# Gated mix of linear attention and a Fourier layer: q' as seven products of quarters, x's forms made once

## The chip, the core and the metric

The kernel runs on one core of a Trainium2 chip. Five engines work side by side: TensorE (PE, matmuls; PEld is its weight load), VectorE (DVE), ScalarE (ACT), GpSimd (POOL) and SyncE (SP). SP and POOL issue nearly all transfers here. Times are device microseconds from runs on the chip; lower is better. What is asked: by how much the change moves the time of 729.68 us.

## The reference

With S = 2048 rows, D = 576 columns, H = 32 heads of 18 columns:

```python
g = sigmoid((x * gate_w).sum(-1, keepdims=True))
q, k, v = split((x @ wqkv))                    # heads of 18
phi = lambda t: where(t > 0, t + 1, exp(t)) + 1e-6
kv  = einsum("bhsd,bhse->bhde", phi(k), v)
z   = einsum("bhsd->bhd", phi(k))
o   = einsum("bhqd,bhde->bhqe", phi(q), kv) / (phi(q) . z + 1e-6)
a   = o.reshape(S, D) @ wo
b   = Cr @ (x @ Wr.T) - Ci @ (x @ Wi.T)        # real part of the 2-D DFT, given as matrices
out = g * a + (1 - g) * b
```

All is fp32. The kernel holds fp32 accuracy in fp32r matmuls: each operand is split into a high part (rounded by a copy) and a low part (the difference), and a product is high x high + high x low + low x high, three passes.

## The kernel before

The rows of x lie in 16 tiles of 128 (NT); D is 4 full chunks of 128 and a rest of 64, whose rows are stored twice so that two passes do for it instead of three. A plain product of one tile and half of the columns (HALF = 288) is therefore 4 x 3 + 2 = 14 matmuls (`steps`, line 272).

The stages, in order of time:

1. **k'** (lines 445 to 562). phi(x Wk) for 16 tiles, in halves. The first four tiles (FT) go through the chunks together while the weights arrive (L502); the other twelve tile by tile (`k_half`, L206 for the matmul). `feature` (L341) takes each half out of its bank: Relu and Exp on ScalarE (L343, L344), an addition on VectorE (L345). `k_split` (L462) splits the tile to high and low (L464). x arrives as `xraw` (L259) and is split by `split_next` (`hi_of`, L176, on ScalarE; `lo_of`, L186, on VectorE).
2. **Attention sums** (lines 565 to 674). G = x^T phi(k), L626, in 20 steps of 4 tiles; kv from Wv and G (`kv_step`, L608 and L611); z from the sum of the phi(k) (`z_chain`, `z_sum`).
3. **q'** (`q_tile`, L677). 16 tiles x 2 halves x 14 matmuls. x is loaded and split a second time. Wq has two more columns, the gate's; `q_tile` takes the gate from the bank of the second half. Beside it run `normalise` (L696, the denominators and the division), `build_m` (L762, M = kv Wo) and `move_m`.
4. **The M stage** (lines 1109 to 1143). Each tile of the attention output is transposed by TensorE (`transposed`, L724), split, multiplied by M in 28 matmuls, scaled by the gate (L1116) and stored as `att`.
5. **Spectral part** (`Hidden.run`, L899, then `sequence`, L1010; twice, for the real and the imaginary matrix). Its products use a scheme of seven products of quarters in place of eight: x of two tiles (p and p + 8) and W are cut to quarters, sums of quarters are formed, and seven products give four quarters of the result. The seven left operands are called the forms of x, the seven right ones the forms of W. A product of forms is 2 x 3 + 1 = 7 matmuls (L896).

The forms of x are made by `Left` (L352): load four quarters, four sums, high and low parts, store to DRAM (`xforms`, L386). Nine of them (8 pairs and the rests) are made here and there: four in k', two in the attention sums, three in the M stage. The forms of W come from `right` (L402), which makes them in three pieces and stores them in DRAM; `Hidden.load_w` (L861) loads them again.

The order: VectorE and ScalarE follow the program text (`pace`), SP too. TensorE's order was left to the framework's planner up to the spectral part and follows the text from there (line 1181). Work that shall come later in the text is kept in lists (`pending`, `tick`). PSUM has eight banks of 512 columns (`bank`).

Of the kernel before, what the change touches and what calls it, by code (L numbers as in the profile page):

```python
# [30 lines left out]

# [15 lines left out]

# [27 lines left out]
QH = HALF, HALF + 2  # L75


LAY_Q = dict(xs=(-256, 4864, 9984, 43776), hi=(15104, 20864), lo=(26688, 31296))
# [3 lines left out]
ORDER = (3, 2, 7, 6, 1, 4, 5)  # L82
MIX_AT = ACC_AT
# [3 lines left out]
XF = 4 * P * 4  # L87


class Layout:  # L90

# [43 lines left out]
def kernel(  # L135
# [6 lines left out]
    wq: bass.AP,  # L142
    wv: bass.AP,
# [35 lines left out]
    pending, paced = [], ExitStack()  # L179

# [67 lines left out]
    raws, split = [], []  # L248
    order = []
    xs_ring = Ring(0, 0, 0)  # L250

    def new_xs(name="xs", ring=xs_ring):
        o = ring.next()
        return (at(o, [P, 10, P], R, name), at(o + XS // 2, [P, 5, P], F, "xraw"))

    def load_next():
        if order:
            xs, raw = new_xs()
            nc.sync.dma_start(out=raw, in_=xa[order.pop(0)])  # L259
            raws.append((xs, raw))  # L260

    def split_next(lo_of=lo_of):
        if raws:
            xs, raw = raws.pop(0)
            hi_of(xs[:, 0:5], raw)
            lo_of(xs[:, 5:10], raw, xs[:, 0:5])
            split.append(xs)

    def x_at(lay):
        xs_ring.at, xs_ring.n = [SLOT_AT + o for o in lay["xs"]], 0  # L270

# [8 lines left out]

    def split_wide(t, c, raw):
        hi_of(t[:, c], raw)
        if c < KC:
            lo_of(t[:, 5 + c], raw, t[:, c])
        else:
            lo_of(t[64:, c], raw[64:], t[64:, c])
# [3 lines left out]
    class Wide:  # L290
# [6 lines left out]
        def load(self, h, pieces=(KC,), queues=None, also=lambda k: None):  # L297
# [5 lines left out]
            for k in pieces:  # L303
                o = self.start + self.lay["lo"][h] + c * n * 4
                los.append((c, at(o, [P, k, n], R, "wd"), at(o, [P, k, n], F, "wraw")))
                c += k
# [9 lines left out]
        def split(self, h, n=1, lo_of=lo_of):  # L316

            hi, los, rest = self.got[h]
            for c, lo, raw in los:
                k = lo.shape[1]  # L320
                m = max(k * n // KC, 1)
                for a in range(0, k, k // m):
                    cs = slice(a, a + k // m)
                    hs = slice(c + a, c + a + k // m)
                    hi_of(hi[:, hs], raw[:, cs])
                    lo_of(lo[:, cs], raw[:, cs], hi[:, hs])
                    yield
            hi_of(hi[:, KC], rest)
            lo_of(hi[64:, KC], rest[64:], hi[64:, KC])
            yield  # L330
# [8 lines left out]
    es = Ring(Y_AT, 1184, 3)  # L339

    def feature(dst, ps):  # L341
        e = at(es.next(), [P, HALF], F, "e")
        nc.scalar.activation(e, ps, AF.Relu, scale=-1.0)  # L343
        nc.scalar.activation(e, e, AF.Exp, scale=-1.0)  # L344
        nc.vector.scalar_tensor_tensor(dst, ps, 0.0, e, op0=ALU.max, op1=ALU.add)  # L345


# [4 lines left out]
    class Left:  # L352

        def __init__(self, k, start, after):
            self.k = k
            if k < NP:
                self.f, self.c = (at(start, [P, 7, 2, 2 * P], d, "xb") for d in (F, R))
                for i in range(2):  # L360
                    begin_after(nc.gpsimd.dma_start(out=self.f[:, 4 * i + 1:4 * i + 3, 1],
                                                    in_=xq[k, :, 2 * i:2 * i + 2]), after)
# [3 lines left out]
            for i in range(4):  # L366
                begin_after(nc.gpsimd.dma_start(
                    out=self.f[:, (1, 2, 5, 6)[i], 1],
# [116 lines left out]
    for _ in range(3):  # L485
        load_next()
# [792 lines left out]
```

## Time and profile before

| what | us |
|---|---|
| three runs | 729.1, 729.68, 730.55 |
| median | 729.68 |
| span of the profiled execution (first to last instruction) | 727.9 |
| PE busy in it | 723.1 |
| DVE busy | 600.3 |
| ACT busy | 335.5 |
| POOL busy | 57.1 |

The profiled execution has no time of its own besides its span; the median of the runs is 1.8 us above the span. In the profile, a busy time is the time in which an engine worked on at least one instruction. Instructions of one engine may overlap a little, so a sum of durations can be above the busy time. A chain of waits is followed back from the last instruction to what released each step. Bytes in the issues are KB of one transfer.

### The profile page before, as it was taken

How to read it: one execution, taken by the hardware profiler on the slowest of the kernel's cores; microseconds unless marked ns; L12 is line 12 of the kernel's file. 1: busy time of each engine (PE TensorE's matmuls, PEld its weight loads, DVE VectorE, ACT ScalarE, POOL GpSimd, SP SyncE). 2: the span in 40 equal slices, each digit the busy share in tenths (PEclk: the TensorE clock that was granted, in tenths of full speed). 3: DMA queues.
4: the chain of work that ended last, by engine and by line, in shares of the span. 5: the costliest groups of instructions: out<-in, count | busy, mean ns of one | idle time of the engine just before them, and what ended most of it. 6: DMA issues, size and time to landing. Idle time of an engine off the chain costs nothing.

```text
span 727.9 us, 13874 instructions
## 1 busy us (share of the span) xinstructions
PE 723.1 (99%) x5446; PEld 722.0 (99%) x5446; DVE 600.3 (82%) x994; ACT 335.5 (46%) x521; POOL 57.1 (8%) x98
## 2 busy tenths in 40 slices
PE   9999999999999999999999999999999999999997
PEld 9999999999999999999999999999999999999997
DVE  5689877689999948989989989857889988788884
ACT  6898346678643544453434333323435322232330
POOL 1011300051132110000000000000000000000000
PEclk9999999999999999999999999999999999999999
DMA  7376796676477999644475666889954443544440
GB/s 255 91 274 220 266 332 199 221 219 230 147 257 279 365 331 380 182 163 144 147 263 168 225 233 199 306 281 402 377 206 135 168 148 124 163 151 140 152 152 33
DMA packets 54228, 158.83 MB, mean 218 GB/s; under 512 B 6412, under 2 KB 10828, under 8 KB 53140
## 3 DMA queue, kind: packets, MB, share of 16 engines
q1 hardware_dynamic: 44916, 118.90, 48.2%
q0 software_dynamic: 8960, 38.65, 14.6%
q8 instruction: 43, 0.70, 0.4%
q10 hardware_dynamic: 288, 0.41, 0.2%
q14 instruction: 21, 0.17, 0.1%
HBM read 115.06 MB, written 41.39 MB: 215 GB/s over the span
## 4 chain that ended last, share of the span: by engine, by line
PE 99%; DVE 0%; DVEq 0%; issue 0%; POOL 0%; POOLq 0%
PE bank L1051 49%; PE bank L206 23%; PE bank L896 14%; PE bank L626 8%; PE bank L502 2%; PE bank L731 1%; PE bank L232 1%; PE bank L608 0%; DVE row L1067 0%; PE bank L611 0%; DVE ys L196 0%; DVEq L1275 0%; POOL ones_f L228 0%; POOL ident masks.py:197 0%; DVEq L1067 0%
## 5 line engine op out<-in xcount | busy, mean ns | idle before, releaser
L1051 PE MATMUL bank<-fh,c 128*128 128x288 f32 x1792 | 357.4, 295 | 0.0
L1051 PEld LDWEIGHTS bank<-fh,c 128*128 128x128 f32 x1792 | 287.3, 188 | 0.1
L1051 PE MATMUL bank<-fl,c 128*128 128x288 f32 x896 | 264.3, 295 | 0.0
L176 ACT ACTIVATE c<-craw 128x1792 fp32r<-128x1792 f32 (+1 forms) x84 | 121.6, 1447 | 188.2 <-DVE craw L196 167.5
L1051 PEld LDWEIGHTS bank<-fl,c 128*128 128x128 f32 x896 | 168.9, 188 | 0.3
L186 DVE TENSOR_TENSOR c<-craw,c 128x1792 fp32r<-128x1792 f32 (+4 forms) x86 | 142.0, 1654 | 2.8 <-ACT c L176 2.6
L196 DVE TENSOR_TENSOR craw<-craw 128x256 f32<-128x256 f32 (+1 forms) x192 | 98.4, 513 | 24.2 <-DMA craw<-in_ci_dram 12.7
L206 PE MATMUL bank<-wd,xs 128*128 128x288 f32 (+1 forms) x784 | 105.9, 296 | 0.0
L206 PEld LDWEIGHTS bank<-wd,xs 128*128 128x128 f32 x784 | 104.6, 188 | 0.1
L896 PE MATMUL bank<-wf,xf 128*128 128x288 f32 x588 | 91.8, 296 | 0.0
L896 PEld LDWEIGHTS bank<-wf,xf 128*128 128x128 f32 x588 | 84.0, 189 | 0.0
L206 PE MATMUL bank<-mw,qs 128*128 128x288 f32 x448 | 63.2, 297 | 0.0
L626 PE MATMUL bank<-pk,c 128*128 128x288 f32 x448 | 60.8, 296 | 0.0
L206 PEld LDWEIGHTS bank<-mw,qs 128*128 128x128 f32 x448 | 59.9, 188 | 0.2 <-DVE qs L186 0.2
L626 PEld LDWEIGHTS bank<-pk,c 128*128 128x128 f32 x448 | 59.9, 189 | 0.0
L196 DVE TENSOR_TENSOR ys<-bank,ys 128x288 f32<-128x288 f32 x63 | 28.8, 457 | 17.1 <-PE bank L1051 14.0
L345 DVE SCALAR_TENSOR_TENSOR acc<-bank,e 128x288 f32<-128x288 f32 x64 | 28.2, 454 | 17.6 <-ACT e L344 12.2
L186 DVE TENSOR_TENSOR fl<-fl,fh 128x864 fp32r<-128x864 f32 (+1 forms) x32 | 34.7, 1094 | 6.7 <-ACT fh L176 5.4
L176 ACT ACTIVATE fh<-fl 128x864 fp32r<-128x864 f32 (+1 forms) x32 | 29.8, 949 | 16.3 <-DVE fl L196 16.3
L896 PE MATMUL bank<-wf,xr 96*128 96x288 f32 x112 | 33.3, 297 | 0.0
L1116 ACT ACTIVATE acc<-bank,gate 128x288 f32<-128x288 f32 x32 | 16.1, 502 | 35.0 <-PE bank L206 34.8
L196 DVE TENSOR_TENSOR ys<-ys,bank 128x288 f32<-128x288 f32 x47 | 21.2, 450 | 13.0 <-PE bank L1051 12.5
(107 smaller groups left out, 664.8 us busy)
## 6 DMA issues: line engine op xcount, KB each, us to landing
xf<-xm SPq DMA_DIRECT2D x42, 512.0 KB, 8.9
craw<-in_cr_dram SPq DMA_DIRECT2D x32, 512.0 KB, 4.0
craw<-in_ci_dram SPq DMA_DIRECT2D x32, 512.0 KB, 3.5
xraw<-in_xa_dram SPq DMA_DIRECT2D x28, 320.0 KB, 3.4
xm<-xb POOLq DMA_DIRECT2D x8, 1024.0 KB, 6.4
wf<-wm SPq DMA_DIRECT2D x14, 576.0 KB, 5.1
xr<-xr SPq DMA_DIRECT2D x14, 448.0 KB, 8.3
xm<-xb POOLq DMA_DIRECT2D x8, 768.0 KB, 5.8
```

Source lines behind the costliest of these rows:

```text
L176: return nc.scalar.activation(dst, src, AF.Copy, bias=bias)
L186: nc.vector.tensor_tensor(out=dst, in0=src, in1=hi, op=ALU.subtract)
L196: nc.vector.tensor_tensor(out=dst, in0=a, in1=b, op=op)
L206: nc.tensor.matmul(ps, a, b, start=(n == 0), stop=(n == len(pairs) - 1))
L232: nc.tensor.matmul(warm[:, :P], ones_f, ones_f, start=True, stop=True)
L345: nc.vector.scalar_tensor_tensor(dst, ps, 0.0, e, op0=ALU.max, op1=ALU.add)
L502: nc.tensor.matmul(ps[i], x[:, i * P:(i + 1) * P], wkt.row(h, j), start=(c == 0 and n == 0), stop=(c == KC and n == 1))
L626: nc.tensor.matmul(ps[h][:, :HALF], t[:, a, k], pk[s][:, b, half(h)], start=(s == 0 and n == 0), stop=(s == NT - 1 and n == len(passes) - 1))
L731: nc.tensor.transpose(banks[c // KC][:, (c % KC) * P:(c % KC + 1) * P], a, ident)
L896: nc.tensor.matmul(ps, a, b, start=(start and n == 0), stop=(n == len(ops) - 1), skip_group_check=True)
L1051: nc.tensor.matmul(ps[q], c[x][:, l, k], factors[p](y, f), start=(p == 0 and i == 0), stop=(p == NP - 1 and i == 2))
L1116: done.append(nc.scalar.activation(acc[i][:, half(h)], ps[:, :HALF], AF.Copy, scale=gate[:, i:i + 1]))
```

## The change

* x's forms are all made once and serve k', q' and the spectral part. For pairs 2 to 7 this is done in the k' stage: `load_left` loads four quarters and the rest of a pair, `make_plain` makes four sums and splits eight forms, and k' itself takes the plain quarters among them (`plain`). The forms of pairs 0 and 1 and of the rests are made in the attention sums and stay in the local memory for q' and the first spectral product.
* q' is seven products of quarters for each pair of tiles (`q_product`), in the order 1, (3 of the pair before), 2, 6, 5, 7, 4. Products 1, 6 and 7 add up in one bank, 5 and 3 in another; ScalarE copies the sum after 1, after 6 and after 7, VectorE adds copies and banks to the quarters, and `tail` applies phi.
* The forms of Wq and of Wr are made in the place where they are used (`pieces`), without a way through DRAM. Wi's still go by `right`.
* The gate's two columns move from Wq to Wk; the gate is taken in k'.
* Work beside TensorE is given to slots: `soon(f, n)` puts f to the n-th next `slot()`, which stands in the text behind each half tile, product or 12 matmuls; `chain` puts a list to successive slots; `plan` ties other work to a step. TensorE follows the text from the k' stage on (`pace(mybir.EngineType.PE)`).
* In the M stage the halves of a transposed tile's split stand behind the first and second half of the tile before; all seven forms of Wr are made there in slots 6 to 19.
* Layouts of the inputs on the host follow (order of tiles TILES, order of the quarters), and places in the local memory change.

```diff
+TILES = [t for p in range(NP) for t in (p, p + NP)]
+A22, A11, A12, S4, S3, S2, S1 = range(7)
+LEFTS = {1: A11, 2: A12, 3: S4, 4: A22, 5: S1, 6: S2, 7: S3}
...
+    def soon(f, n=1, rank=1):
+        due.setdefault(clock[0] + n, []).append((rank, f))
+    def chain(*fs, at=1):
+        for n, f in enumerate(fs):
+            soon(f, at + n)
+    def slot():
+        clock[0] += 1
+        for _, f in sorted(due.pop(clock[0], ()), key=lambda rf: rf[0]):
+            f()
...
+        def make_plain(self, raw, both):
+            r, c = self.of[:, :, 1], self.all
+            quarters, others = slice(0, 4), slice(4, 8)
...
+            return [
+                lambda: next(sums),
+                lambda: next(sums),
+                lambda: (hi(quarters), hi_of(both[:, 0], raw)),
+                lambda: (lo(quarters), lo_of(both[:, 1], raw, both[:, 0]), hi(others)),
+                lambda: (lo(others), self.store(slice(0, 4)), self.store(slice(4, 7))),
+            ]
...
+    def pieces(src, rest, groups, raw_at, queue):
...
+        def raws(r):
+            add(r(3), r(5), r(0), ALU.subtract)
+            add(r(5), r(2), r(5), ALU.subtract)
+            yield
+            add(r(4), r(2), r(3), ALU.subtract)
+            add(r(6), r(4), r(1), ALU.subtract)
+            yield
+        def piece(c, after):
+            loads = [queue.dma_start(out=place[f][1][:, 2 * c + 1], in_=src[c][:, q])
+                     for q, f in enumerate((0, 5, 1, 2))]
...
+            yield from raws(lambda f: place[f][1][:, 2 * c + 1])
+            late = []
+            for t, raw, fs in where:
+                n = (len(fs) + 1) // 2 if len(fs) > 4 else len(fs)
+                for k in range(0, len(fs), n):
+                    ks = slice(k, min(k + n, len(fs)))
+                    hi_of(t[:, ks, 2 * c], raw[:, ks, 2 * c + 1])
+                    for f in late:
+                        f()
+                    late = [lambda t=t, raw=raw, ks=ks: lo_of(
+                        t[:, ks, 2 * c + 1], raw[:, ks, 2 * c + 1], t[:, ks, 2 * c])]
+                    yield
...
+    def load_left(p):
+        left = Left(p, SLOT_AT + p % 3 * FORMS, queue=nc.sync)
...
+    pace(mybir.EngineType.PE)
...
-    for i in range(FT, NT):
-        xs = split.pop(0)
-        k_half(i, 0, xs)
...
+    def plain(c, both, i, rhs):
+        for k, f in enumerate((1 + A11, 1 + A12) if i < NP else (0, 1 + A22)):
+            for a in range(2):
+                j, cs = 2 * k + a, slice(a * P, a * P + P)
+                yield c[:, f, 0, cs], rhs(j)
+                yield c[:, f, 0, cs], rhs(5 + j)
+                yield c[:, f, 1, cs], rhs(j)
+        yield both[:, 0, i // NP], rhs(4)
+        yield both[:, 1, i // NP], rhs(4)
+
+    for p in range(FT // 2, NP):
+        c, both, _ = ahead.pop(p)
+        if 4 < p + 2 < NP:
+            load_left(p + 2)
+        for n, (i, h) in enumerate((i, h) for i in (p, p + NP) for h in range(2)):
+            ps = bank()[:, :GATED[h]]
+            run(ps, plain(c, both, i, lambda j: wkt.row(h, j)))
+            if p + 2 < NP and n == 3:
+                chain(*ahead[p + 2][2])
+            if p + 1 == NP and n % 2 == 0:
+                xg_next()
+            slot()
+            k_feature(i, h, ps)
...
-    def q_tile(i):
-        xs = split.pop(0)
...
-            run(ps, steps(xs, lambda j: wqt.row(h, j)))
...
+    def quarter(i, h, a, b, op=ALU.add):
+        c = acc[i][:, half(h)]
+        add(c, a, b, op)
+        tail(c)
...
+    def q_product(p, q):
+        b = q_banks.setdefault(p, {})
+        name = {1: "a", 6: "a", 7: "a", 2: "b", 4: "c", 5: "e", 3: "e"}[q]
+        start = q in (1, 2, 4, 5)
+        if start:
+            b[name] = bank()[:, :HALF]
+        ps, x, w = b[name], q_x[p], wq_forms[PRODUCTS[q][1]]
+        ops = [(x[:, LEFTS[q], a, c * P:c * P + P], w[:, 2 * c + d])
+               for c in range(2) for a, d in FULL]
+        ops.append((q_rest[p][:96, LEFTS[q]], w[:96, 4]))
+        for n, (l, r) in enumerate(ops):
+            nc.tensor.matmul(ps, l, r, start=(start and n == 0), stop=(n == len(ops) - 1),
+                             skip_group_check=True)
+        slot()
+        if q in (1, 6, 7):
+            b[q] = at(s_ring.next(), [P, HALF], F, "s")
+            soon(lambda: nc.scalar.activation(b[q], ps, AF.Copy), rank=0)
+        if q == 2:
+            soon(lambda: quarter(p, 0, ps, b[1]), rank=0)
+        elif q == 7:
+            soon(lambda: quarter(p + NP, 1, b["e"], b[7]), 2, rank=0)
+        elif q == 4:
+            soon(lambda: quarter(p + NP, 0, b[7], ps, ALU.subtract), rank=0)
+        elif q == 3:
+            soon(lambda: quarter(p, 1, ps, b[6]), rank=0)
...
+    order = [(p, q) for p in range(NP) for q in (1, 2, 6, 5, 7, 4)]
+    for p in range(NP):
+        order.insert(order.index((p + 1, 2)) if p + 1 < NP else len(order), (p, 3))
...
+    for n in range(4):
+        plan((4 + n // 2, (6, 7)[n % 2]), split_m, n // 2, n % 2)
...
+    for p in range(2, NP):
+        for k in ((p - 1, 3), (p, 2), (p, 6), (p, 5)):
+            plan(k, go, norms)
...
+    for n in range(14):
+        plan(6 + n, lambda n=n: go(wq_parts[n // 5]))
...
+    for k in range(2 * NT):
+        plan(k, go, norms, 2)
     for i in range(NT):
-        qs = nxt
+        qs = nxt[0]
         if i + 1 < NT:
             nxt = transposed(i + 1)
+        t = TILES[i]
         for h in range(2):
             ps = bank()
             run(ps[:, :HALF], steps(qs, lambda j: m_row(h, j)))
...
+            if i + 1 < NT:
+                nxt[1 + h]()
+            slot()
...
-    paced.enter_context(tc.manual_schedule(engines={mybir.EngineType.PE}))
```

More of the change, by code (lines that the diff above doesn't have):

```diff
@@ L245 @@
     acc = [at(ACC_AT + i * D * 4, [P, D], F, "acc") for i in range(NT)]
[L248 to L270, printed above, removed]
     def steps(xs, rhs):
@@ L567, with gates @@
+    def gates():
+        nc.vector.tensor_scalar(gate, gate, 1.0, None, op0=ALU.add)
+        nc.vector.reciprocal(out=gate, in_=gate)
+    soon(gates, 3)
+    WV_AT = C_AT + 4 * 2 * CU * P * 4
+    ZB_AT = WV_AT + 2 * XD
     zacc = at(K_AT + 2 * XD, [P, D], F, "zacc")
@@ L621 @@
             t = xg_split.pop(0)
+            if step:
+                xg_load()
+            xg_next()
+            if q == 1:
+                chain(*wv_split)
+            if q == 3 and c < 4:
+                wvt[c + 1], wv_split = load_pair(wv_ring.next(), wv[:, c + 1])
+            if step == 11:
+                z_sum()
             for k in range(CU):
```

691 lines of the change are left out of this document (390 added, 301 removed).

## The prediction

> **What bounds the kernel now.** I read four views in this order: the page's first lines, the waits of TensorE, the chain of work that ended last, and the busy time by stage. From the page, the waits of PE, and the chain (start us, duration us, what):
>
> ```profile
> span 727.9 us, 13874 instructions
> PE 723.1 (99%) x5446; PEld 722.0 (99%) x5446; DVE 600.3 (82%) x994; ACT 335.5 (46%) x521; POOL 57.1 (8%) x98
> ...
> PE bank L232 <- POOL ones_f L228: 1.2, 1, 1.2
> ...
> 19.97 44.55 PE bank L206 x336
> ...
> 128.88 3.75 PE bank L206 x28
> ...
> 133.59 49.30 PE bank L206 x370
> ...
> 183.44 7.57 PE bank L206 x56
> ...
> 191.55 6.89 PE bank L206 x52
> ...
> 236.76 0.55 PE bank L731 x5
> 237.30 3.71 PE bank L206 x28
> ...
> 262.03 52.52 PE bank L896 x392
> ```
>
> TensorE is busy 723.1 of 727.9 us, its one recorded wait is 1.2 us at the start, and the chain is TensorE from end to end. A busy PE could still be a slow one, so I divide the pieces by their matmuls: k' tiles 44.55/336 = 132.6 ns each, the products of the spectral stage 52.52/392 = 134.0 ns. The stages differ by 1%: PE runs at one pace, with nothing hidden in its busy time but a few tenths of a microsecond. So time here is the number of matmuls times about 133 ns, plus whatever stops PE. The kernel gets faster only by fewer matmuls, and slower as soon as an engine behind PE no longer keeps up. How near they are to that, by stage (the stretch; busy PE, PEld, DVE, ACT, POOL; clock, DMA share, GB/s):
>
> ```profile
> 19.81:64.50 44.69, 44.69 (x340) 44.69 (x339) 36.70 (x67) 40.06 (x84) 5.18 (x8) 1.00 0.61 207
> 64.50:97.50 33.00, 33.00 (x253) 33.00 (x252) 27.32 (x46) 15.36 (x26) 8.05 (x12) 1.00 0.74 260
> 97.50:133.60 36.10, 36.10 (x282) 36.10 (x281) 24.95 (x42) 20.70 (x40) 1.08 (x2) 1.00 0.80 272
> 133.60:182.90 49.30, 49.30 (x372) 49.30 (x372) 40.62 (x96) 38.62 (x96) 13.04 (x22) 1.00 0.63 197
> 182.90:262.00 79.10, 79.10 (x610) 78.79 (x609) 71.14 (x144) 40.63 (x88) 17.17 (x28) 1.00 0.76 267
> ```
>
> These are k', the attention sums (two rows), q' and the stage that multiplies o by M (the M stage below). VectorE is 82%, 76%, 82% and 90% busy there, and PE loses no time to it. The clock is 1.00.
>
> **What the change takes away.** Before, q' is 16 tiles x 2 halves x 14 matmuls = 448. After, it is 8 pairs of tiles x 7 products x 7 matmuls = 392. No other count changes: k' keeps 14 a half (the new `plain` yields 4 x 3 + 2), and the attention sums, M and spectral stages keep theirs. The pieces from 128.88 to 198.44 hold 28 + 370 + 56 + 52 = 506 matmuls of line 206: the 448 of q', 30 of build_m, 28 of the first M tile. They take 3.75 + 49.30 + 7.57 + 6.89 = 67.51 us, 133.4 ns each, so q' costs 448 x 133.4 = 59.8 us. The new products have the very shape of the spectral ones, seven matmuls of 288 columns, the last of 96 rows, and the chain shows 392 of those: 52.5 us. The gate's two columns move from 224 q' matmuls to 224 k' matmuls, 2/288 of 133 ns each, 0.2 us. **Net: 59.8 - 52.5 - 0.2 = 7.1 us less on the path.** With the k' pace for the products it would be 59.8 - 52.0 - 0.2 = 7.6.
>
> **What it adds and moves, stage by stage.** All the rest lies beside PE and is free only while it fits under PE. VectorE's durations by form, then four of its instructions in order of time:
>
> ```profile
> L345 DVE SCALAR_TENSOR_TENSOR acc<-bank,e 128x288 f32<-128x288 f32 x64 | 28.2, 454 | 17.6 <-ACT e L344 12.2 <-DMA xr<-xb 5.3
> L464 DVE SCALAR_TENSOR_TENSOR pk<-acc,pk 128x576 fp32r<-128x576 f32 x16 | 12.0, 755 | 1.9 <-ACT pk L176 1.5
> L196 DVE TENSOR_TENSOR xb<-xb 128x256 f32<-128x256 f32 x36 | 14.3, 422 | 0.3
> L186 DVE TENSOR_TENSOR xb<-xb,xb 128x1024 fp32r<-128x1024 f32 x9 | 11.0, 1221 | 10.6 <-ACT xb L176 10.6
> L709 DVE SCALAR_TENSOR_TENSOR acc<-acc,den 128x576 f32<-128x576 f32 x16 | 12.1, 754 | 0.3
> L702 DVE TENSOR_REDUCE den<-pz 128x32 f32<-128x576 f32 x16 | 12.1, 753 | 0.5
> L701 DVE SCALAR_TENSOR_TENSOR pz<-acc,zb 128x576 f32<-128x576 f32 x16 | 12.0, 752 | 0.0
> L706 DVE RECIPROCAL den<-den 128x64 f32<-128x64 f32 x8 | 4.4, 553 | 0.3
> L714 DVE COPY twice<-acc 128x128 f32<-128x128 f32 x16 | 3.8, 236 | 0.6
> L705 DVE TENSOR_SCALAR den<-den 128x64 f32<-128x64 f32 x8 | 1.8, 231 | 0.2
> L186 DVE TENSOR_TENSOR qs<-bank,qs 128x512 fp32r<-128x512 f32 x16 | 11.0, 685 | 1.3 <-ACT qs L176 1.2
> L186 DVE TENSOR_TENSOR qs<-bank,qs 128x128 fp32r<-128x128 f32 x16 | 4.5, 282 | 0.0
> L186 DVE TENSOR_TENSOR wb<-wb 128x1152 fp32r<-128x1152 f32 x4 | 5.4, 1352 | 0.0
> L186 DVE TENSOR_TENSOR wb<-wb 128x864 fp32r<-128x864 f32 x4 | 4.2, 1052 | 0.0
> ...
> 45.01 0.46 DVE L345 SCALAR_TENSOR_TENSOR acc<-bank,e 128x288 f32<-128x288 f32 x1
> 45.38 0.76 DVE L464 SCALAR_TENSOR_TENSOR pk<-acc,pk 128x576 fp32r<-128x576 f32 x1
> 46.05 0.46 DVE L345 SCALAR_TENSOR_TENSOR acc<-bank,e 128x288 f32<-128x288 f32 x1
> 46.41 0.82 DVE L186 TENSOR_TENSOR xs<-xraw,xs 128x640 fp32r<-128x640 f32 x1
> ```
>
> The last four start 0.37, 0.67 and 0.36 us apart while they last 0.46, 0.76 and 0.46: where nothing is waited for, an instruction of VectorE costs its duration less 0.09 us. I use that, and keep the full duration as the other end.
>
> k' stage. Each pair of tiles needs 4 tails of phi (L345), 2 splits of k' (L464) and, new, the eight forms of one pair of x: 4 sums and a remainder's difference of 256 columns, 2 differences of 1024. Full durations: 4 x 0.454 + 2 x 0.755 + 5 x 0.422 + 2 x 1.221 = 7.88 us; less 13 x 0.09 it is 6.71. PE takes 56 x 132.6 ns = 7.43 us for a pair. So 90%: it fits, and the forms are due two halves after the last sum, so a lag of a microsecond is not seen. The old k' splits of x (12 of 640 columns, L186 above) go in exchange.
>
> Attention sums. VectorE was busy 27.32 + 24.95 = 52.3 of 69.1 us. In come one more set of x's forms (4 x 0.422 + 1.221 + about 0.95 for 768 columns = 3.9), four late splits of k' (3.0), and Wq's seven forms, which I price at the 13.3 worked out below for Wr's, against some ten differences of 288 columns for its plain split (4.5). Out go three splits of x (0.82 each, 2.5) and three of Wo (2.3). That makes 63.3, 92%, and what PE needs is due a step of 24 matmuls (3.2 us) later: it fits.
>
> q' stage. PE takes 49 x 134.0 ns = 6.57 us for a pair. VectorE has 4 additions out of banks and 4 tails, all at L345's 0.454, and, from the third pair on, four of the nine steps of a `normalise`, which is 2 x (0.752 + 0.753 + 0.754 + 0.236) + 0.231 + 0.553 = 5.77 us in ten instructions. 8 x 0.454 + 5.77 x 4/9 = 6.20 us; less 12.4 x 0.09 it is 5.08, 77%. In pairs 4 and 5 two splits of M of 576 columns (0.755 as L464) are added: 7.71 full, 6.41 spaced, just under 6.57. Removed: q's second split of x.
>
> M stage. A tile takes PE 0.55 + 3.71 = 4.26 us. VectorE has the transposed tile (0.685 + 0.282), 4 steps of normalise (2.57), and over seven tiles the forms of Wr: two pieces of 4 sums (0.454), 1.352 and 1.052, and a last one that I price as 4 sums, five 288-column differences and one of 576 (0.454, 0.755): 8.44 + 4.84 = 13.3, 1.90 a tile. Sum 5.44; less 9.5 x 0.09 it is 4.58. That is **over** PE's 4.26, by 0.32 x 7 = 2.2 us in all. The cover is the lead: a tile's lower half can start about 1.5 us into the tile before (0.55 for the transposes and at most 0.97 on ScalarE, taken as long as VectorE's 0.685 + 0.282), takes 0.97, and is due at 4.26 + 0.55 = 4.81. That leaves 2.3 us against 2.2. It fits by nothing to spare.
>
> New waits inside PE's order. Product 6 adds onto the bank that ScalarE copies after product 1, and 7 onto the one copied after 6. Between 1 and 6 stand two products; between 6 and 7 only one. One product is 7 x 134 = 0.94 us. ScalarE's rows for the parts:
>
> ```profile
> L343 ACT ACTIVATE e<-bank 128x288 f32<-128x288 f32 x64 | 25.7, 401 | 10.2 <-PE bank L206 8.3 <-PE bank L502 1.8
> L344 ACT ACTIVATE e<-e 128x288 f32<-128x288 f32 x64 | 28.5, 445 | 2.0
> ...
> L896 PE MATMUL bank<-wf,xf 128*128 128x288 f32 x588 | 91.8, 296 | 0.0
> ```
>
> A matmul ends 0.296 us after it starts, 0.16 after the next one starts; the copy takes 0.40 as L343. So ScalarE has 0.94 - 0.16 - 0.40 = 0.38 us to spare. Behind the copy nothing else of PE waits, and the written order puts the copy first in its slot. ScalarE is 3 x 0.40 + 4 x (0.401 + 0.445) = 4.6 of 6.57 us busy.
>
> DMA. Each pair's eight forms are loaded (512 KB and 128 KB) and stored in k' instead of in three stages; Wr's forms are not stored and loaded any more, which frees the M stage. Issues (KB, us to landing):
>
> ```profile
> xm<-xb POOLq DMA_DIRECT2D x8, 1024.0 KB, 6.4
> ...
> xm<-xb POOLq DMA_DIRECT2D x8, 768.0 KB, 5.8
> ...
> xb<-in_xq_dram POOLq DMA_DIRECT2D x16, 256.0 KB, 3.8
> ```
>
> 640 + 1792 KB is 2.49 MB in 7.43 us, 335 GB/s. The M stage moved 267 GB/s at a share of 0.76, which is 351 at a full share. So k' would run its DMA at about 95%. A load waits for the store of the pair three before it (same place): about 6.4 + 1 us for the store, 4 to 5.5 for the load, against two pairs, 14.9 us.
>
> **The sum.** 727.9 - 7.1, and for small stalls 0.2 us in each of the four stages, since VectorE's margins are 10% or less and in M nil: 0.8, between 0 and the rivals. Span 721.6. The median shown is 729.68, 1.8 above the profiled span, and that stays: **723.4 us**, 0.9% less. With no stall and 7.6 saved it would be 722.1, with 3 us of stalls 725.6.
>
> **Rivals.**
> 1. VectorE becomes the bound (the slower one). If its instructions cost full durations: k' 7.88 - 7.43 = 0.45 x 6 pairs = 2.7 us; q' pairs 4 and 5, 7.71 - 6.57 = 1.1 x 2 = 2.3; M (5.44 - 4.26) x 7 - 2.3 = 6.0. Together 11.0: 729.7 - 7.1 + 11.0 = 733.6 us. From 8.6 us on the kernel is slower than before. For it: three stages near 90% at once, and an order in which ScalarE's and VectorE's instructions wait in line behind each other. Against it: the 0.09 us, seen in every pair of rows above, and a stage M that already ran 90% without loss. The Trainium skill, page "VectorE: DVE Perf Modes", section "The DRAIN you can't avoid", says the next instruction does not start until the pipe is empty; by it full durations might add up, which is this rival's 733.6. The trace speaks against it, with starts 0.37 us apart for 0.46 us instructions. 10%.
> 2. The bank of product 7 is late. If ScalarE stands in a Relu and Exp (0.85) when product 6 ends, the copy comes up to 0.85 - 0.38 = 0.47 us late, 8 times: 3.8 us, 727.2. For it: ScalarE 70% busy and VectorE's additions ahead of its tails. Against: those tails can run a slot early. 12%.
> 3. Forms of x late by DMA in k'. At the k' stage's own full-share rate, 207/0.61 = 339 GB/s, pairs take 7.35 us, still under 7.43; at 267, the rate the M stage really had, 9.3: 1.9 us for each of the three pairs that wait for a place, 5.7, so 729.1: no change. 8%.
> My forecast, 722.1 to 725.6, has 68%; 2% are left for less than that.
>
> **Range and chances.** Low 721.6, high 729.0: forecast and rival 2, with most of rival 3. About 0.2% (1.5 us) is what a measurement of this kernel tells from no change. Faster: the forecast, most of rival 2 and what lies below, 0.80. Same: rival 3 and the small end of rival 1, 0.09. Slower 0.11.
>
> **What would show it.** 5390 matmuls on PE's line; q' as 392 in some 52.5 us; no waits of PE above a few tenths. If rival 1 holds, PE waits for VectorE on the forms in k' and on the transposed tiles in M, with DVE at its full share there; if 2, PE waits for ScalarE's copies eight times, evenly; if 3, VectorE's first sums wait for DMA in k'. The forecast is wrong if PE's waits after the start exceed 3 us.

## The result, and the profile after

| kernel | median us (lowest to highest) | runs | ratio to before, 95% interval |
|---|---|---|---|
| before | 729.39 (728.46 to 730.55) | 4 | |
| after | 737.47 (734.59 to 738.54) | 4 | 1.0105 [1.0083, 1.0127] |

The change makes the kernel 1.1% slower; 723.4 us was forecast. The profiled execution of after took 734.59 us, 1.7 above its span of 732.9, at a granted clock of 1.000. The other three have spans of 735.3 to 736.8 us at 0.995 to 0.998, so the median stands 2.9 us above the profiled run.

First the page of after, then its list of TensorE's waits (engine, line, what it waited for: us in total, times, longest).

```profile
span 732.9 us, 13678 instructions
PE 718.7 (98%) x5390; PEld 715.2 (98%) x5390; DVE 596.8 (81%) x991; ACT 331.5 (45%) x530; POOL 54.2 (7%) x101
...
PE 73%; DVE 11%; ACT 6%; DMA 5%; issue 3%; POOL 1%; DVEq 0%; POOLq 0%; ACTq 0%; SPq 0%
```

```profile
PE bank L785 <- DVE c L180: 3.5, 4, 1.6
PE bank L785 <- ACT plain L157: 2.0, 1, 2.0
PE bank L785 <- ACT c L157: 1.4, 1, 1.4
PE bank L226 <- POOL ones_f L222: 1.2, 1, 1.2
PE bank L200 <- DVE qs L180: 0.8, 1, 0.8
PE bank L838 <- DVE acc L190: 0.4, 2, 0.2
PE bank L200 <- DVE xb L180: 0.4, 1, 0.4
PE bank L685 <- DVE gt L180: 0.3, 1, 0.3
```

The 5390 matmuls are there, 56 fewer than before. But the chain, PE from end to end before, now runs through VectorE, ScalarE and transfers for 22% of the span. PE has eleven waits after the start, 8.8 us by this list; 6.9 of them are on line 785, the attention sums. By stage (k', sums, q', M, cut at the first matmul of each; columns as in the windows of before):

```profile
19.81:66.28 46.47, 46.08 (x345) 45.84 (x344) 39.23 (x73) 38.59 (x92) 6.58 (x12) 1.00 0.81 301
66.28:139.04 72.76, 65.84 (x494) 64.24 (x493) 56.03 (x95) 34.58 (x62) 15.36 (x26) 1.00 0.76 264
139.04:198.87 59.83, 58.98 (x441) 58.03 (x440) 48.02 (x108) 44.25 (x112) 8.43 (x16) 1.00 0.69 238
198.87:268.00 69.13, 68.17 (x525) 67.70 (x524) 53.82 (x114) 33.00 (x77) 13.68 (x25) 1.00 0.44 150
```

Busy PE is below the stretch's length by 0.39, 6.92, 0.85 and 0.96 us. The sums took 72.8 us; before they reached from 64.5 to 128.9, 64.4 us. From the start of q' to the end of M it is 128.96 us, before 262.03 - 128.88 = 133.15: 4.2 less, where the products alone should give 7.3.

That closes. The forecast without stalls was 727.9 - 7.1 = 720.8. The missing busy time is 9.1 us; a matmul is drawn 0.16 us past the start of the next, so each of eleven waits is that much longer than listed, 1.8. In the first 6.5 us PE did 24 matmuls and not 30 (two rows below, after and before), 0.8. 720.8 + 9.1 + 1.8 + 0.8 = 732.5, against 732.9. **The 7 us were saved, and 11 us of new waits were paid.**

```profile
0.00:6.50 6.50, 5.30 (x24) 5.30 (x25) 1.95 (x4) 3.00 (x5) 1.59 (x10) 1.00 0.72 230
```

```profile
0.00:6.50 6.50, 5.30 (x30) 5.13 (x31) 2.06 (x4) 3.00 (x5) 1.59 (x10) 1.00 0.73 235
```

Where a wait comes from is read in the order of time. The first (timeline of after: start, duration, engine, line, operation, and in brackets the idle time before and what ended it):

```profile
72.56 1.35 POOL L325 DMA_DIRECT2D xb<-in_xq_dram  x2 [9.82 <-ACT c L157]
...
78.05 0.76 DVE L190 TENSOR_TENSOR xb<-xb 128x256 f32<-128x256 f32 x2 [1.31 <-DMA xb<-in_xq_dram]
...
80.31 1.06 ACT L157 ACTIVATE xb<-xb 128x1024 fp32r<-128x1024 f32 x1 [5.54 <-DVE xb L190]
...
81.60 1.07 PE L785 MATMUL bank<-pk,c 128*128 128x288 f32 x6 [1.58 <-DVE c L180]
```

The sums begin at 66.28. The load of pair 0's quarters, written at slot 0, is issued only at 72.56, because `begin_after(done[-1])` ties it to a split on ScalarE. VectorE reaches the first sum and stands there 1.31 us. ScalarE, which needs that sum, stands 5.54 us. Behind them in their lines are the two halves of the next tile of x (`c`), which have nothing to do with pair 0, and for that tile PE waits 1.58 us. Both engines stood idle in the microseconds before PE had to wait for them. The second place:

```profile
99.06 1.21 POOL L477 DMA_DIRECT2D wraw<-in_wq_rest_dram  x2 [8.14 <-ACT c L157]
100.38 2.18 POOL L453 DMA_DIRECT2D wf<-in_wq_dram  x4
...
102.95 6.81 SPq L396 DMA_DIRECT2D xr<-xb  x6
...
106.63 1.09 POOL L453 DMA_DIRECT2D wf<-in_wq_dram  x2 [1.00 <-issue]
...
109.88 1.42 SPq L598 DMA_DIRECT2D craw<-in_xg_dram  x1
...
113.78 1.89 ACT L157 ACTIVATE wf<-wraw 96x2016 fp32r<-96x2016 f32 x1 [4.17 <-DMA wf<-in_wq_dram]
...
115.70 2.25 DVE L180 TENSOR_TENSOR wf<-wraw,wf 32x2016 fp32r<-32x2016 f32 x1 [5.96 <-ACT wf L157]
...
117.30 0.63 ACT L157 ACTIVATE c<-craw 128x512 fp32r<-128x512 f32 x1 [1.04 <-DMA craw<-in_xg_dram]
...
117.98 0.81 PE L785 MATMUL bank<-pk,c 128*128 128x288 f32 x4 [1.36 <-ACT c L157]
...
120.32 0.93 PE L785 MATMUL bank<-pk,c 128*128 128x288 f32 x5 [1.53 <-DVE c L180]
...
133.67 2.36 PE L785 MATMUL bank<-pk,c 128*128 128x288 f32 x16 [2.00 <-ACT plain L157]
```

The split of Wq's rest reads `wraw`, which is there, but waits for the last of Wq's loads, which write other parts of the tile it writes. They too are held, and issued up to 107.7 us. Behind that split ScalarE then waited 1.04 us for the tile of x itself, whose load was issued at 109.88 and took 7.4 us to land. So PE's wait at 118 has two late transfers ahead of it, Wq's and the tile's. From 105 to 115 us the transfers ran at their full share (next row), the rests' six stores of 448 KB among them.

```profile
105.00:115.00 10.00, 10.00 (x80) 10.00 (x79) 3.35 (x7) 2.45 (x4) 1.70 (x4) 1.00 1.02 389
```

VectorE and ScalarE were busy 3.35 and 2.45 of these ten microseconds, just ahead of PE's waits for them.

### The profile page after: what moved, and what is told of

Same layout as the page of the kernel before. It is cut to its first block, busy times and chain, and to the rows that moved or that the text cites. A ratio compares the mean times of both kernels' runs of the same rounds, so it can differ in the third digit from the quotient of the medians.

```text
span 732.9 us, 13678 instructions
## 1 busy us (share of the span) xinstructions
PE 718.7 (98%) x5390; PEld 715.2 (98%) x5390; DVE 596.8 (81%) x991; ACT 331.5 (45%) x530; POOL 54.2 (7%) x101
## 4 chain that ended last, share of the span: by engine, by line
PE 73%; DVE 11%; ACT 6%; DMA 5%; issue 3%; POOL 1%; DVEq 0%; POOLq 0%; ACTq 0%; SPq 0%
PE bank L1264 48%; PE bank L1110 14%; PE bank L200 5%; PE bank L838 5%; DMA xb<-in_xq_dram 2%; ACT xb L157 2%; DVE wf L180 1%; DVE xb L180 1%; DVE xb L190 1%; DMA wraw<-in_wk_dram 1%; ACT wf L157 1%; DMA wf<-in_wq_dram 1%; DMA craw<-in_xg_dram 1%; ACT e L306 1%; DVE pz L862 1%
## 5 line engine op out<-in xcount | busy, mean ns | idle before, releaser
L200 PE MATMUL bank<-wd,xb 128*128 128x288 f32 (+1 forms) x288 | 42.6, 296 | 0.4 <-DVE xb L180 0.4
L200 PEld LDWEIGHTS bank<-wd,xb 128*128 128x128 f32 x288 | 39.8, 189 | 0.6 <-DVE xb L180 0.6
L838 PE MATMUL bank<-wf,xq 128*128 128x288 f32 x252 | 39.6, 296 | 0.3 <-DVE acc L190 0.2
L838 PEld LDWEIGHTS bank<-wf,xq 128*128 128x128 f32 x252 | 35.8, 189 | 0.8 <-DVE acc L190 0.8
L190 DVE TENSOR_TENSOR fl<-bank,y 128x288 f32<-128x288 f32 x48 | 21.7, 451 | 13.3 <-ACT y L1137 8.7
```

Of the source, the lines that this page charges most:

```text
L190: nc.vector.tensor_tensor(out=dst, in0=a, in1=b, op=op)
L200: nc.tensor.matmul(ps, a, b, start=(n == 0), stop=(n == len(pairs) - 1))
L838: nc.tensor.matmul(ps, l, r, start=(start and n == 0), stop=(n == len(ops) - 1), skip_group_check=True)
```

## The experiments

My theory, after this: **late arrivals**, each with two engines in line behind it. Rivals: VectorE's amount of work; the transfer rate; the order of TensorE, which the change takes from the planner and leaves to the text. All medians, each against the kernel before on the same chip (729.3 to 729.7):

| run | median us | ratio, 95% interval |
|---|---|---|
| e1_left | 733.84 | 1.006 [1.0037, 1.0083] |
| e2_wq | 734.66 | 1.0077 [1.0051, 1.0103] |
| e4_noz | 736.84 | 1.0089 [1.0064, 1.0114] |
| e5_m | 736.40 | 1.0103 [1.0065, 1.0142] |
| e6_all | 732.93 | 1.004 [1.0023, 1.0057] |
| f1_spread | 730.38 | 1.0016 [1.0005, 1.0028] |
| f2_plan | 741.25 | 1.0162 [1.0142, 1.0182] |
| g1_rate | 737.38 | 1.0094 [1.0061, 1.0126] |
| f4_late | 730.31 | 1.0004 [0.9982, 1.0027] |
| f5_apart | 729.73 | 0.9999 [0.9978, 1.002] |
| f6_pace | 732.81 | 1.0034 [1.0022, 1.0047] |
| f7_order | 732.93 | 1.0042 [1.0026, 1.0058] |
| f8_third | 728.60 | 0.9989 [0.9975, 1.0002] |
| f9_sp | 729.19 | 0.9995 [0.9984, 1.0005] |
| f10_early | 728.97 | 0.9989 [0.9977, 1.0001] |
| f11_sp3 | 734.55 | 1.0068 [1.0054, 1.0082] |
| f12_fifth | 727.78 | 0.9973 [0.9962, 0.9983] |

**e1_left**: the loads of x's forms in the sums are not held.

```diff
-        left = made[k] = Left(k, o, done[-1])
+        left = made[k] = Left(k, o)
```

> The loads of the forms of x made in the attention sums (pair 0, the rests, pair 1) are not held back for a ScalarE instruction any more; each starts as soon as its place is free. Theory (late transfers): VectorE's first sum no longer waits for pair 0's quarters at 78 us, TensorE's waits of 1.7 + 0.3 + 0.4 us between 79 and 89 us go, and the attention sums shrink from 72.8 to about 70.5 us; time about 735. Rival (amount of work on VectorE): VectorE was late anyway with sums of z, forms and late splits in the same stretch; the waits move by at most 0.5 us and the time stays at 737. Rival (DMA rate): the earlier load takes rate from k' and the waits return there; time 736.5 to 738.

3.6 us below after. The POOL row for pair 0's load moves from 72.56 to 62.25 us, and PE's waits there shrink to 0.2 us each. Wq's loads, still held, go out earlier too (95.2 to 101.8 us, in after 99.1 to 107.7), since the stage lags less, and the waits at 118 and 120 are one of 0.5. The longest is now one of 3.2 us, for `ACT plain`, at the end of the sums.

**e2_wq**: Wq's loads are not held.

```diff
-    plan(16, lambda: begin(2, wq_last(done[-1])))
+    plan(16, lambda: begin(2, wq_last(None)))
...
-        plan(16, lambda k=k: begin(k, wq_piece(k, done[-1])))
+        plan(16, lambda k=k: begin(k, wq_piece(k, None)))
```

> Wq's ten loads are not held back for a ScalarE instruction any more. Theory (late transfers): they start about 4 us sooner (95 in place of 99 us), ScalarE's wait of 4.2 us before the split of Wq's rest goes, TensorE's waits of 1.5 + 1.7 us at 116 to 120 us go, and the 2.2 us at 131, a consequence of the lag, at least halves; attention sums 68.5 to 70, time about 733.5. Rival (amount of work): VectorE and ScalarE then only get through the stage as before; under 1 us gained, time 736.5 or more. Rival (DMA rate): the stretch from 103 to 118 us moves all it can already, so the last of the ten lands as late as before and the wait stays.

2.8 us below after. The split of Wq's rest now follows its sums at once (106.25 us), and the waits at 118 and 120 are gone. In their place ScalarE waits for tiles of x, and behind that PE's clock falls (timeline, then windows, of e2_wq):

```profile
112.84 0.63 ACT L157 ACTIVATE c<-craw 128x512 fp32r<-128x512 f32 x1 [4.10 <-DMA craw<-in_xg_dram]
...
125.13 0.63 ACT L157 ACTIVATE c<-craw 128x512 fp32r<-128x512 f32 x1 [4.22 <-DMA craw<-in_xg_dram]
```

```profile
125.00:130.00 5.00, 3.23 (x16) 2.88 (x16) 1.85 (x3) 4.87 (x9) 1.04 (x2) 0.75 0.47 182
130.00:135.00 5.00, 3.14 (x13) 3.17 (x14) 5.00 (x11) 0.97 (x2) 1.08 (x3) 0.50 0.93 349
135.00:140.00 5.00, 5.00 (x32) 5.00 (x31) 2.93 (x5) 1.95 (x3) 0.54 (x1) 0.73 0.98 397
```

What was late changed its name: freed transfers meet others.

**e4_noz**: less work for VectorE in the same stage; fourteen of the fifteen additions that sum phi(k) are left out.

```diff
-    for n, ops in enumerate(at_z):
+    for n, ops in enumerate(at_z[:1]):
```

> Fourteen of the fifteen additions that sum phi(k) for z are left out (z is the sum of two tiles only): 14 x 0.67 = 9.4 us less on VectorE in the first 15 of the 40 slots of the attention sums, with every load as it was. Rival (amount of work on VectorE): the waits of TensorE at 79 to 89 us (2.4 us) go, and those at 116 to 133 shrink since VectorE is no longer behind; time 732 to 734. Theory (late transfers): VectorE and ScalarE stand at the same loads; the waits at 79 us stay within 0.5 us, those at 116 us too; but Wq's loads, which overwrite the tiles that these additions read, are still held by ScalarE, so nothing moves; time 736 to 738.

0.6 us below after, inside the spread of either. Fourteen additions at 0.67 us from start to start, 9.4 us of VectorE's time, bring next to nothing in the time. The waits did move, further than the theory allowed: the one that ended at 82 us fell from 1.58 to 0.65 and the one that ended at 134 from 2.00 to 0.28, so additions that stand between a late load and the tile behind it lengthen a wait. But the one that ended at 120 grew from 1.53 to 2.07, with a clock of 0.76 and 0.56 in the two stretches of 5 us from 115 on, and q' has new waits of 1.1 and 1.4. The amount has a share in single waits; the time does not follow it.

**e5_m**: in the M stage, Wr's rests first and the steps spread.

```diff
-    for n in range(14):
-        plan(6 + n, lambda n=n: go(wq_parts[n // 5]))
+    for n, k in enumerate([2] * 4 + [0] * 5 + [1] * 5):
+        plan(6 + 2 * n if n < 9 else 15 + n, lambda k=k: go(wq_parts[k]))
```

> Wr's forms are made in slots 6 to 28 of the M stage, the rests first and at most one step in two slots, in place of slots 6 to 19. VectorE's work there stays the same, spread over 23 slots. Theory for the M stage (VectorE is crowded in slots 6 to 19): TensorE's waits of 0.3 and 1.0 us at 238 and 247 us go, the M stage shrinks by 1.2 to 1.5 us, time 736. Rival (the transposed tile's chain itself is late, its lower half stands behind other work of its slot): the waits stay, spread over more tiles; time 737 to 738.

The wait for `DVE qs` is no longer in PE's list, so the M stage's 1.3 us are of this order; the median falls by only 1.1, within its spread, since the sums' waits and lower clocks (0.992 to 0.995) lie over it. Up to the M stage this is the program of after, and the profile fell on one of its slowest executions (740.01 us). It has waits of 1.1 and 1.5 us in q' that the profile of after, taken in its fastest execution, doesn't have; e4 and g1, with the same q' products, have the 1.4 and 1.5 too. The slower executions of after may well lose time there as well; no profile of one exists.

**e6_all** and **f1_spread**: the three together; then also the stage's other transfers spread.

```diff
...
-    plan(21, lambda: made[NP].store_rest())
+    for n in range(3):
+        plan(22 + 3 * n, lambda n=n: made[NP].store_rest((n,)))
...
-    plan(30, load_q_rest, 0)
-    plan(32, load_q_rest, 1)
-    plan(27, load_forms, 2)
+    plan(34, load_q_rest, 0)
+    plan(36, load_q_rest, 1)
+    plan(33, load_forms, 2)
```

> Neither x's forms nor Wq's quarters are held back in the sums, and Wr's forms take the rests first and are spread out in the M stage (the three edits tried alone, together). Late arrivals, each with engines standing in line behind it: the three gains were 3.6, 2.8 and 1.1 us of 737.5 and have different places, so together 730.0, and no stall above 0.5 us at 79, 116 or 246. Transfer rate: what is begun earlier meets at 100 to 130 us at the full rate, the waits move from Wq's quarters to the tiles of x, and PE keeps two stalls of 2 to 3 us there with a fall of the clock behind them: 732 to 734.

> As the three edits together, and the stage's transfers that nothing waits for moved out of 100 to 118 us: the rests' store (six of 448 KB on SP's queue, at slot 21 at once) goes in three parts of two at slots 22, 25 and 28, the forms of the third pair are fetched at slot 33 and not 27, the rests at 34 and 36 and not 30 and 32. Transfer rate: the tiles of x come in time, no stall above 0.5 us from 95 to 135 us, and the time falls by 2 to 4 us below the three edits together, to 726 to 729. Late arrivals alone (not the rate): within 0.7 us of the three edits together.

4.5 us below after and not 7.5. The waits at 79, 116 and 246 us went, and two of 2.6 and 3.2 us came at 125 and 130, behind a tile of x for which ScalarE stood 5.2 us, as the transfer rate had it. But the three gains did not have different places to begin with: e1 alone had taken most of the waits at 118 and 120, e2's place. Spreading brings 2.6 more, within the 2 to 4 of that theory, and ends at 1.0016 of before, above its 726 to 729, with a wait of 1.7 us left at 126. So is it the rate? **g1_rate** is the spreading alone, with the loads held as in the change.

> The changed kernel with the spread transfers alone (the rests' store in three parts at slots 22, 25, 28; the rests fetched at 34 and 36; the forms of pairs 2, 3, 4 at slot 37 and in q'), x's forms and Wq's quarters held back as in the change. Transfer rate as the main cause: the stalls at 116 to 119 and 131 (5.4 us) and in q' (0.9 us) shrink to a third, those at 79 to 88 (2.7 us) stay: 731 to 733. Late issue as the main cause (the holding back): Wq's ten loads are still issued late and the stalls at 79 and 116 to 119 stay; only 131 and q' improve: 734 to 736.

737.38: no gain at all, above both expectations. Held loads are the first cause; what f1 spreads counts only once they are issued in time. Whether it then counts by the rate or by the order on SP's queue, which f1 changes too, these runs do not separate.

**f2_plan**: TensorE's order up to the spectral part is the planner's again.

```diff
-    pace(mybir.EngineType.PE)
+    pace()
...
+    paced.enter_context(tc.manual_schedule(engines={mybir.EngineType.PE}))
     first.load_rest(4)
```

> The changed kernel, with TensorE's order up to the spectral part left to the planner, as in the kernel before, and no longer that of the text. Order theory: before, other matmuls could go ahead of one whose operand was late, and that is what is gone; with it back PE's stalls in the sums fall by half and more and the time is 731 or less. Late arrivals: in the sums each product of PE needs what is late, there is little to go ahead of, and the time is that of the changed kernel within 1.5 us (736 to 739).

3.8 us slower than after, which neither theory had. By its trace PE's waits in the sums fall from 6.9 to 3.3 us, by half and more as the order theory had it, but 7.2 us of waits stand between 139 and 203 us, where after has 0.7. The planner moves other work with it, so the run doesn't isolate the order: the text's order may have a share in the sums' waits, and the planner's costs more than that in q'.

**f4_late, f5_apart**: the forms of pairs 2 to 4 fetched later in the text; then also pair 0's steps at every second slot.

```diff
-    plan(33, load_forms, 2)
-    plan(36, load_forms, 4)
-    plan(38, load_forms, 3)
+    plan(37, load_forms, 2)
...
+    plan((0, 4), load_forms, 3)
+    plan((1, 2), load_forms, 4)
```

> As the spread version, and the eight forms of pairs 2, 3 and 4 (1.75 MB each, on POOL's queue) are fetched at slot 37 of the sums, and within products 4 of pair 0 and 2 of pair 1, and not at slots 33, 38 and 36. Transfer rate: from 120 to 148 us the tiles of x, the rests and Wo's first three groups no longer share the full rate with 5 MB that is needed 15 us later; the stalls at 126 (1.9 us) and at 136 to 146 (2.5 us) fall to a quarter: 726.5 to 727.8. If those stalls are not of the rate (SP's order, or ScalarE's line), they stay and the time is 729.8 to 731.

> As f4_late, and the five steps that make pair 0's forms stand at slots 3, 5, 7, 9 and 11 of the sums and not at 3 to 7. VectorE runs without a gap from 74 to 87 us there, with the additions of z between; PE's three small stalls (0.34, 0.32, 0.39 us at 79, 83 and 87) are then of VectorE's amount and order: 0.6 to 1.0 us below f4_late. If they are of something else: no difference (within 0.4 us).

f4 does nothing, and f5's timeline says why:

```profile
124.36 3.26 POOL L707 DMA_DIRECT2D xq<-xm  x6 [12.41 <-DMA craw<-in_xg_dram]
...
127.82 3.14 PE L784 MATMUL bank<-pk,c 128*128 128x288 f32 x16 [2.45 <-ACT plain L157]
...
147.31 0.68 ACT L157 ACTIVATE plain<-wraw 126x576 fp32r<-126x576 f32 x1 [2.35 <-DMA wraw<-in_wo_dram]
...
148.34 1.06 PE L837 MATMUL bank<-wf,xb 128*128 128x288 f32 x6 [1.32 <-ACT s L842]
```

All six pieces of three pairs go out at 124 us, though four of them are written within q', which begins at 134.7: a later line in the text does not make GpSimd wait, only a wait does. 5 MB then run beside Wo's groups; ScalarE stands 2.35 us for one of these, and behind it is the copy that PE waits for. The expectations call it product 7's; counted from the start of q' it is the copy after product 1 of pair 1, and the product that waits is 6. f5's small waits at 79 to 87 us did go, with no clear gain in the median (0.6, the spreads overlap).

**f6_pace, f7_order**: the forms of pairs 3 and 4 wait for Wo's third group; then Wq's steps from slot 18 and pair 1's forms a slot later.

```diff
-        return t, (lambda: hi_of(t[:n, 0], raw[:n]), lambda: lo_of(t[:n, 1], raw[:n], t[:n, 0]))
+        return t, (lambda: done.append(hi_of(t[:n, 0], raw[:n])), lambda: lo_of(t[:n, 1], raw[:n], t[:n, 0]))
...
+            if after:
+                begin_after(d, done[-1])
...
+    plan((0, 3), load_forms, 3, True)
+    plan((1, 5), load_forms, 4, True)
```

> As f5_apart, with the fetches of the forms of pairs 3 and 4 made to wait for the first half (the part for TensorE) of Wo's third group. In f4_late and f5_apart all six pieces of pairs 2 to 4 were issued at 124 us whatever their place in the text, since nothing made GpSimd wait. If it is the transfer rate, Wo's first three groups land 3 to 8 us sooner, ScalarE no longer holds product 7's copy behind them, the stalls at 142 and 147 us (2.5 us) fall under 0.6: 727.5 to 728.3. If Wo's groups are late for another reason (they are issued at 133 us only), the stalls stay and the time is 729.3 to 730.2.

> As f6_pace, with the steps of Wq's forms from slot 18 on and not 20, and pair 1's forms at slots 35 to 39 and not 34 to 38. The stall left in the sums (2.6 us at 125) is one of line: the last tiles of x take TensorE 2.1 us each and not 3.2, and ScalarE and VectorE come to them by turns behind the last forms of Wq. If so, it falls under 1 us: 1.5 to 2.5 us below f6_pace, near 725.5. If the tile is late itself (its place in the ring of four), no difference.

In f6 the waits at 142 and 147 went as expected, in f7 the one at 125 as well (for one of 1.0 at 107, the copy of the sum of z). But M's moves on GpSimd's queue now stood behind the 3.5 MB, up to 5.0 us each, and PE took new waits at 165 and 173 us (1.4 and 2.9): 3 us slower than f5. Only the second is behind M's moves (VectorE stands 2.6 us for `mraw`); the first is for a rest of x, on SP's queue.

**f8_third, f9_sp, f10_early**: only pair 4 waits; pair 4 on SP's queue; Wq's steps from slot 18 and the sum of z earlier.

> As f7_order, but only the forms of pair 4 wait for Wo's third group, those of pair 3 do not; Wq's steps from slot 19 on; the sum of z one step earlier. Late transfers: in f6 and f7 the moves of M (from slot 145 to 165 us on GpSimd's queue) stood behind 3.5 MB of forms, hence the stalls at 165 and 173; with half of it they shrink under 1.5 us together, those at 106, 125 and 147 stay under 0.6 each: 726 to 728, faster than before. If the stalls are the price of the seven products, they show up elsewhere again and the time is 729 to 732.

> As f8_third, with pair 4's forms fetched on SP's queue and not GpSimd's, so that M's moves stand behind no forms at all. Queue order: the stalls at 165 and 173 are gone, 725 to 727. Transfer rate (the same bytes at the same time): no better than f8_third, within 0.7 us.

> As f9_sp, with Wq's steps from slot 18 on (where f7_order had lost the stall at 125 us) and the sum of z made at slots 14 to 19, ahead of the rests' split, so that its copy doesn't stand behind that (the 1.2 us at 106 in f7_order). If line and late transfers were all that the change cost: no stall above 0.7 us, the granted clock at 0.999 or more in most runs, 724 to 726, which is below before and near the forecast's sum. If there is a price of the seven products besides: 728 to 729 as f8 and f9.

Spans of 726.1 to 727.5 us in the profiles, 728.6 to 729.2 in the median: below before in each, by less than can be told, and above what was expected in all three. In f9 the waits at 165 and 172 are down to 0.7 and 0.2, as queue order had it; f8 still has 1.8 at 172. f8 and f9 keep one wait of 2.3 and 2.8 us at 125, and most of their other runs a clock of 0.995 to 0.999; f10 loses it and has one of 1.2 at 145 instead, again for the copy after pair 1's product 1, behind Wo's groups. f10's median lies where its expectation put a price of the seven products besides, but its trace needs none: eight waits of 3.9 us after the start, longer by 0.16 each, are 5.2, and 720.8 + 5.2 + 0.8 = 726.8, against a span of 727.5. **f11_sp3** sends pair 3 on SP's queue too, with the wait.

> As f10_early, with the forms of pair 3 also waiting for Wo's third group, and on SP's queue. Late transfers: the stalls at 140 to 147 us (2.5 us) fall under 0.9, M's moves on GpSimd's queue stand behind nothing, and the time falls by 1 to 2 us to 727 to 728, faster than before by over 0.2%. If the forms of pair 3 then come late themselves, a stall of 1 us or more at 155 to 160, and the time stays at 728.5 to 729.5.

Neither: the waits at 140 to 147 went, but a wait of 5.9 us, ending at 170, came (timeline and windows of f11):

```profile
143.60 2.15 SPq L707 DMA_DIRECT2D xq<-xm  x4
...
152.34 6.86 SPq L716 DMA_DIRECT2D xr<-xr  x2
...
170.24 0.61 PE L839 MATMUL bank<-wf,xr 96*128 96x288 f32 x1 [5.91 <-DMA xr<-xr]
```

```profile
165.00:170.00 5.00, 0.00 (x0) 0.00 (x0) 0.00 (x0) 0.00 (x0) 0.00 (x0) 0.95 1.04 347
170.00:175.00 5.00, 4.76 (x20) 4.76 (x21) 2.44 (x6) 2.85 (x7) 0.00 (x0) 0.50 1.00 390
175.00:180.00 5.00, 5.00 (x35) 5.00 (x35) 4.18 (x8) 2.95 (x7) 0.00 (x0) 0.87 0.09 34
```

A rest of 448 KB, issued at 152.3, lands 18 us later behind 5.2 MB of forms on one queue, and every engine stands still. **f12_fifth** issues pair 5's forms behind it.

```diff
-    plan((1, 4), load_forms, 5)
+    plan((2, 5), load_forms, 5)
```

> As f11_sp3, with the forms of pair 5 fetched within product 5 of pair 2, behind the rest of pair 4 on SP's queue and not ahead of it. Queue order: the rest lands within 6 us of its issue at 152, the 6 us at 164 go, nothing above 0.7 us is left, and the time is 725.5 to 727.5, faster than before by over 0.2%. If the rate alone was short (150 to 175 us ran at the full rate in f11), a stall of 2 us or more stays at 160 to 170: 730 to 732.

727.78 us, 0.9973 [0.9962, 0.9983] of before: faster than both kernels, though 0.3 above the expected range. The rest of pair 4 still lands 12.9 us after its issue and not within 6, and PE waits 1.0 for it. Its page and its list of PE's waits:

```profile
span 727.1 us, 13670 instructions
PE 718.9 (99%) x5390; PEld 715.6 (98%) x5390; DVE 596.3 (82%) x991; ACT 331.5 (46%) x530; POOL 52.0 (7%) x97
```

```profile
PE bank L226 <- POOL ones_f L222: 1.2, 1, 1.2
PE bank L839 <- DMA xr<-xr: 1.0, 1, 1.0
PE bank L786 <- DVE c L180: 0.7, 2, 0.4
PE bank L1267 <- DVE fl L180: 0.6, 1, 0.6
PE bank L786 <- ACT c L157: 0.5, 1, 0.5
PE bank L839 <- DVE acc L190: 0.2, 1, 0.2
```

3.0 us of waits after the start, and VectorE's busy time is what it was in after (596.3 against 596.8). The same products, the same work for VectorE, 9.7 us less: only the times and queues of transfers and the slots of some steps differ. The spans of its eight runs are 725.0 to 727.1 us, 4 to 6 above the 720.8 without any stall; the listed waits with 0.16 for each of six are 4.0. With the 0.8 at the start that gives 725.6 for the profiled execution, 1.5 below its span.

## Why the prediction was wrong

- **What bounds the kernel, and the 7.1 us for 56 matmuls: right.** The sums of the first section close to 0.4 us with it.
- **The step that failed is the attention sums' "it fits".** It priced 63.3 us of VectorE's work in 69.1 and took a lag of a step as harmless. VectorE had less, 56.0 us by the windows row, and PE still lost 6.9 there. I never asked when the held loads land, nor what stands behind the instruction that waits for them. e1, e2 and e4 show it: issuing the loads earlier gives 3.6 and 2.8 us (with places that overlap), taking 9.4 us of work away 0.6. f12 shows it best: with VectorE's work as in after, 9.7 us come back. PE's waits after the start, which were to stay under 3 us, were 8.8.
- **The sum's 0.2 us of stalls a stage** was therefore wrong by place: k' lost 0.4, the sums 6.9, q' 0.9, M 1.0 by the windows.
- **The M stage, "nothing to spare": right mechanism.** One wait of 0.8 for `qs`, 1.3 us of stalls in all where the margin was priced at nil; e5 removes them by order alone.
- **"The median stays 1.8 above the span": wrong**, 4.6. Each execution is some 1.7 us above its own span, much as before; but the profile fell on the fastest of four, and the others have spans of 735.3 to 736.8 us and lower clocks. That their stalls were longer and lowered the clock is likely, not shown.
- **Rival 1 (VectorE the bound)** came nearest to the time, 733.6 against 737.47, but by luck: it put nothing into the sums and 6.0 into M. **Rival 2 (product 7's copy)** did not appear. Where PE, in the text's order, did wait for a copy (1.2 to 1.5 us in e4, e5, g1, f1, f4, f5 and f10) it was product 6 of pair 1, the one with two products between and the larger margin, once, with ScalarE standing behind a late group of Wo; that was not its mechanism. **Rival 3 (forms late by DMA)** had the right kind of cause in the wrong stage: k' lost 0.4 us of the 5.7.

What stays open: the last 4 us of f12's stalls and 1.5 us of its span, the 0.8 us at the start, and why the planner's order in f2 costs q' so much.

## What to carry to other kernels

Where engines take their work in a written order, price a moved step by when its data lands and by what stands behind it on each engine, not by each engine's share; an engine with a quarter of its time free can be the one that is waited for. A load that is tied to another instruction for pacing needs its landing time worked out, and a load that is only written later isn't later. When a late transfer is cured, look at once for what it now runs beside and behind on its queue: in this case each cure made the next wait, until the order on the queues followed the order of need.

## What the hardware showed besides

A stall of TensorE can cost more than its length. In e2_wq, after waits of 2.3 and 2.4 us close together, the granted clock was 0.75, 0.50 and 0.73 in three stretches of 5 us, with 13 to 32 matmuls in each where 38 fit (the second wait lies in the first two). In f11 a wait of 5.9 us was followed by 0.50 and 0.87. f12, with no wait above 1.0 us after the start, has 0.999 to 1.0 in all eight runs; after, with waits up to 2.0, had less in three of four. The Trainium skill, page "TensorE: Matmul & The Clock Gate", section "HAM oscillation — how this bites in real kernels", gives the rule that TensorE should not idle for more than about 3.4 us. Here less was at times enough. In f9_sp a single wait of 2.83 us left the clock at 1.00 in the stretches during and after it, but in f5_apart a single wait of 2.45 us is followed by this (its windows):

```profile
125.00:130.00 5.00, 2.55 (x16) 2.35 (x16) 4.70 (x9) 1.93 (x4) 2.54 (x5) 0.91 0.99 356
130.00:135.00 5.00, 5.00 (x34) 5.00 (x33) 2.96 (x6) 2.11 (x3) 0.00 (x0) 0.75 1.01 417
```
